# Pooled attention and soft MoE on one core: fewer and wider TensorE products, logit sums on VectorE, uneven weight rows moved

## The chip, the cores and the metric

The kernel runs on one core of a Trainium2 chip. The time is the device time of one execution in microseconds (us). A core has TensorE (PE; PEld is its weight load), VectorE (DVE), ScalarE (ACT), GpSimd (POOL), SyncE (SP) and 16 DMA engines, which all the transfers share. Instructions reach TensorE from a program in memory, and the profile lists the transfers that fetch it as a DMA queue of their own.

## The reference, cut to what matters

```python
B, H, S, D = 8, 8, 576, 64          # q, k, v: float32
k_p = k.reshape(B, H, 72, 8, D).mean(axis=3)       # pooled keys, v_p likewise
scores = q @ k_p.T / 8;  attn = softmax(scores, -1)
x = (attn @ v_p) as [4608 tokens, 512]             # heads side by side
logits = x @ phi                                   # phi: 512 x 32 slots
d = softmax(logits, over the 4608 tokens);  slot_input = d.T @ x     # 32 x 512
for e in range(8):                                 # 4 slots per expert
    slot_out[e] = relu(slot_input[e] @ w1[e]) @ w2[e]    # 512 x 1024, 1024 x 512
c = softmax(logits, over the 32 slots);  out = c @ slot_out          # 4608 x 512
```

## The kernel before, in words

**Data and loads.** The batches are taken two at a time: four pairs, `NP = 4`. A partition of a loaded tile holds 72 consecutive tokens of one head of one batch, so a pair's q, k or v fills 128 partitions with 72 x 64 values. All loads but half of the first one are issued by POOL and cast to bf16 on the way. They go in one order through one queue: k, q, phi and v of pair 0, k of pair 1, then q, v and the k after next, with w1 of the experts between them, then w2. `big` has four buffers for q, k and v (line 101), so a load waits until PE has done with the tile that lay there four loads earlier. The later halves of w2 take over the places of `big`, `qTa` and `xsa` when attention has finished with them. `load_w2` (line 115) brings experts 0 to 5 and half of expert 6; the loop at line 446 brings the rest of experts 6 and 7, cut into two column halves with four pieces each. Eight completion semaphores go round the loads that POOL issues: a load waits for the landing of the eighth load before it.

**Attention.** `prepare_kq` pools k: `pool_stage` (line 231) multiplies 8 strided slices by a matrix of 1/8 that keeps the partitions apart, in two parts of 4 and 5 rows of means, so 16 products; ACT copies the means out twice side by side; `turn_stage` (line 244) transposes them into `kp`; line 259 transposes q into `qTa`. `prepare_v` does the same for v, and line 281 multiplies one head's pooled v by `iphi`, the unit matrix beside phi of that head, so that a value row is followed by its share of the 32 logits. `score_unit` computes scores (line 290) and ACT their exponentials (line 292). `u_tile` (line 304) multiplies four heads' exponentials by values, and DVE divides by the sum (lines 309 and 315) into `xsa`. Preparing the next pair is a generator that is stepped between score units.

**Soft MoE.** `dispatch` (line 322) sums the eight heads' shares of the logits by eight products with the unit matrix, takes the exponential (line 323), and adds e x x into `G_ps` (line 326). It runs once per pair inside the next pair's attention, and for the last pair in two parts (tokens 0 to 4 and 5 to 8 of 9) after the loop. Then: `hidden` (line 475), `second_layer` (line 496) by expert as w2 lands, and from `begin` on the combine products (line 554), scaled by ACT (line 527) and DVE (line 529) and stored by SP (line 545).

**Order.** POOL keeps the written order throughout; for the other engines a scheduler orders the attention part, and the last part (from `hidden` on) is in the written order. `warm` (line 141) runs 8 products on zeros near the start.

**Uneven rows.** The load of w1 of expert 0 (line 106) is cut into partitions 0 to 111, 112 to 119 and 120 to 127; the other loads are not cut. A row of it is 4 x 1024 values, 8 KB as it lands.

Of the kernel before, what the change touches and what calls it, by code (L numbers as in the profile page):

```python
# [18 lines left out]
def kernel(  # L19
# [83 lines left out]

    def load_w1(e, n, parts=((0, 128),)):
        for p0, p1 in parts:
            nc.gpsimd.dma_start(out=w1_sb[p0:p1, e:e + n].rearrange("p e j f -> p e (j f)"),
                                in_=moe_w1[e:e + n].rearrange("e (p j) f -> p e (j f)", j=DJ)[p0:p1])

    w2_at = {}

    def load_w2(home, e, n, j0=0, j1=FJ):
# [3 lines left out]
        nc.gpsimd.dma_start(out=home[:, 0:n, j0 * DM:j1 * DM],  # L115
                            in_=moe_w2[e:e + n].rearrange("e (p j) d -> p e j d", j=FJ)[:, :, j0:j1].rearrange("p e j d -> p e (j d)"))

# [20 lines left out]

    def warm(n, ps):
        for _ in range(n):  # L140
            nc.tensor.matmul(out=ps, lhsT=zeros[:, 0:128], rhs=zeros, start=True, stop=True)

    warm_ps = ps_m.tile([128, 512], FP, name="warm_ps", tag="m")
    warm(8, warm_ps)
    dummy = consts.tile([128, 1], BF)
# [14 lines left out]

    iphi = consts.tile([128, H, XW], BF)
    with tc.tile_pool(name="tmp", bufs=1) as tmp:
        col = tmp.tile([128, A], FP, name="col")
        nc.vector.reduce_sum(out=col, in_=ident.rearrange("p (h a) -> p a h", a=A), axis=AX.X)
        head = tmp.tile([128, H], FP, name="head")
        nc.vector.reduce_sum(out=head, in_=ident.rearrange("p (h a) -> p h a", a=A), axis=AX.X)
        sel = tmp.tile([128, J, 2, A, J], BF, name="sel")
        nc.vector.memset(sel, 0.0)
        for j in range(J):
            nc.vector.tensor_copy(out=sel[:, j, :, :, j], in_=col.rearrange("p a -> p () a").to_broadcast([128, 2, A]))  # L170
        for r in range(2):
            rows = slice(r * D, (r + 1) * D)
            nc.vector.tensor_copy(out=iphi[rows, :, 0:D],
                                  in_=ident[rows, rows].rearrange("p d -> p () d").to_broadcast([D, H, D]))
# [9 lines left out]
        nc.scalar.copy(out=iphi[:, :, D:XW], in_=phi_ps)  # L184
    nc.vector.memset(siT, 0.0)
# [40 lines left out]
    def pool_stage(src, means, done):  # L226

        for i, (r0, r1) in enumerate(PARTS):
            ps = ps_m.tile([128, r1 - r0, D], FP, name="pool_ps", tag="m")
            for t in range(POOL):  # L230
                nc.tensor.matmul(out=ps, lhsT=pmat, rhs=src[:, r0 * POOL + t:r1 * POOL:POOL, :],  # L231
                                 start=(t == 0), stop=(t == POOL - 1))
            if i:
                done()
            nc.scalar.copy(out=means[:, r0:r1],
                           in_=ps.rearrange("p r d -> p r () d").to_broadcast([128, r1 - r0, means.shape[2], D]))
            yield

    def turn_stage(means, dst):
        dst = dst.rearrange("p n (r i) -> p r n i", r=NR)  # L240
        for r0, r1 in PARTS:
            ps = ps_m.tile([means.shape[2] * D, r1 - r0, BH, NI], BF, name="turn_ps", tag="m")
            for r in range(r0, r1):
                nc.tensor.transpose(out=ps[:, r - r0].rearrange("p n i -> p (n i)"),  # L244
                                    in_=means[:, r].rearrange("p c d -> p (c d)"), identity=ident)
            nc.vector.tensor_copy(out=dst[:, r0:r1], in_=ps)
            yield

    def prepare_kq(pair):
# [3 lines left out]
        kp[pair] = kvpool.tile([128, BH, SP], BF, name="kp", bufs=2)  # L253
        yield from turn_stage(means, kp[pair])
        for n, t0 in enumerate(range(0, NU, 6)):
# [14 lines left out]
    def prepare_v(pair):  # L270

        means = kvpool.tile([128, NR, 1, D], BF, name="vmeans")
        yield from pool_stage(v_sb[pair], means, lambda: after_v(pair))
        vpar = kvpool.tile([D, BH, SP], BF, name="vpar")
        yield from turn_stage(means, vpar)
        for b in range(2):
            for qd in range(2):
                ps = ps_m.tile([SP, HQ, XW], FP, name="v_ps", tag="m")
                for hh in range(HQ):
                    h = qd * HQ + hh  # L280
                    nc.tensor.matmul(out=ps[:, hh], lhsT=vpar[:, b * H + h], rhs=iphi[0:D, h], start=True, stop=True)
                nc.scalar.copy(out=vp[(2 * pair + b) % 5][:, qd * HQ:(qd + 1) * HQ, 0:XW], in_=ps)
                yield
# [33 lines left out]

    def dispatch(x, t0, t1, ps, ee):

        lg = ps_m.tile([128, 9, NS], FP, name="lg_ps", tag="m")[:, 0:t1 - t0]  # L320
        for h in range(H):
            nc.tensor.matmul(out=lg, lhsT=ident, rhs=x[:, t0:t1, h, D:XW], start=(h == 0), stop=(h == H - 1))  # L322
        nc.scalar.activation(out=ee[:, t0:t1], in_=lg.rearrange("p t s -> p t () s").to_broadcast([128, t1 - t0, NG, NS]), func=AF.Exp)  # L323
# [93 lines left out]
    load_w2(qTa, 4, 2)  # L417
    load_w2(xsa[:, 0:1], E - 2, 1, 0, CUT6)
    row_sums(0, 20, False)
# [116 lines left out]
    n = 0  # L536
# [99 lines left out]
```

## Time and profile before

| | |
|---|---|
| median of 3 runs | 176.71 us (175.95 to 176.75) |
| profiled execution | 175.6 us, its span 173.8 us |
| mean granted TensorE clock | 0.860 |
| busy: PE, DVE, ACT, POOL | 129.4, 90.9, 83.0, 20.3 us |
| DMA | 41.14 MB landed or stored in 10542 packets |

In the profile, L12 is line 12 of the kernel. A row of a group shows the engine, the operation, the tile written and those read, how often, then busy time, the mean of one in ns, and the idle time before it with what ended it. The page's digits are tenths of a fortieth of the span. An arrow `<-` after an idle time names what ended the wait.

### The profile page before, as it was taken

The page shows a single profiled execution, that of the slowest core. Times are in us where ns is not written, and L with a number is a line of the kernel's source. Part 1 is how long each engine was busy: PE and PEld are TensorE (multiplying, and loading weights), DVE is VectorE, ACT ScalarE, POOL GpSimd, SP SyncE. Part 2 cuts the span into 40 slices and gives each one's busy share as a digit, 9 for nine tenths or more (in the row PEclk, how much of TensorE's full clock was granted, in tenths as well). Part 3 has the DMA queues.
Part 4 walks back from the last instruction along what each step waited for, and adds up shares of the span by engine and source line. Part 5 has one row for each costly group of instructions (what it writes and reads, how often), then busy time and mean ns, then how long its engine had stood idle before and what let it go on. Part 6 is the DMA issues. An engine that isn't in the chain of part 4 may idle for free.

```text
span 173.8 us, 3094 instructions
## 1 busy us (share of the span) xinstructions
PE 129.4 (74%) x1239; PEld 76.9 (44%) x1240; DVE 90.9 (52%) x251; ACT 83.0 (48%) x155; POOL 20.3 (12%) x38
## 2 busy tenths in 40 slices
PE   5205889999999998979998897889973096798000
PEld 2003555766677665756765455534451032332000
DVE  4403242487777879758798668614260002599100
ACT  3200248976767469755698941450120004799000
POOL 7000111132110060100100004041010030000000
PEclk9955799999999999999999995555599569999755
DMA  5999999999999999999999999999999999999995
GB/s 190 246 221 219 218 218 209 218 216 214 218 212 207 216 216 216 214 221 215 215 213 213 215 222 217 217 213 211 217 219 221 202 193 197 308 359 409 437 437 226
DMA packets 10542, 41.14 MB, mean 237 GB/s; under 512 B 785, under 2 KB 6417, under 8 KB 6689
## 3 DMA queue, kind: packets, MB, share of 16 engines
q0 software_dynamic: 7072, 30.48, 86.4%
q1 hardware_dynamic: 3456, 10.49, 15.4%
q8 instruction: 9, 0.15, 0.3%
q14 instruction: 5, 0.03, 0.0%
HBM read 61.93 MB, written 9.44 MB: 411 GB/s over the span
## 4 chain that ended last, share of the span: by engine, by line
DMA 46%; PE 26%; issue 7%; DVE 5%; ACT 5%; POOL 2%; DVEq 0%; POOLq 0%; ACTq 0%
DMA qTa<-in_moe_w_dram 20%; DMA big<-in_q_dram 14%; DMA phi_f<-in_moe_phi_dram 7%; PE pool_ps L231 6%; DMA xsa<-in_moe_w_dram 6%; PE sc L290 5%; PE u_ps L304 4%; DVE w_sb L529 4%; PE q_ps L259 4%; ACT exa L292 3%; PE G_ps L326 2%; PE lg_ps L322 1%; PE turn_ps L244 1%; PE f_ps L554 1%; ACT qTa L263 1%
## 5 line engine op out<-in xcount | busy, mean ns | idle before, releaser
L292 ACT ACTIVATE exa<-sc 72x576 bf16<-72x576 f32 x64 | 39.1, 649 | 11.7 <-PE sc L290 11.3
L315 DVE TENSOR_TENSOR xsa<-u_ps,rec 128x384 bf16<-128x384 f32 x69 | 37.7, 552 | 1.4
L304 PE MATMUL u_ps<-vp,exa 72*128 72x97 bf16 (+1 forms) x320 | 27.1, 221 | 1.4 <-DVE xsa L315 1.3
L290 PE MATMUL sc<-qTa,kp 64*72 64x288 bf16 x128 | 23.2, 304 | 1.8 <-ACT exa L292 1.7
L304 PEld LDWEIGHTS <-exa 72*128 72x128 bf16 (+1 forms) x320 | 17.7, 106 | 10.7 <-DVE xsa L315 3.6
L231 PE MATMUL pool_ps<-big,pmat 128*128 128x320 bf16 (+1 forms) x128 | 20.2, 303 | 0.5 <-DMA big<-in_k_dram 0.5
L309 DVE RECIPROCAL rec<-u_ps 128x4 f32<-128x4 f32 x72 | 12.4, 176 | 15.1 <-PE u_ps L304 14.6
L231 PEld LDWEIGHTS <-pmat 128*128 128x128 bf16 x128 | 12.4, 103 | 5.0 <-DMA big<-in_k_dram 0.6
L259 PE MATMUL q_ps<-ident,big 128*128 128x128 bf16 x144 | 11.7, 219 | 2.3 <-DMA big<-in_q_dram 1.2
L554 PE MATMUL f_ps<-so,cT 128*128 128x512 bf16 (+1 forms) x42 | 10.2, 337 | 1.8 <-ACT w_sb L527 0.8
L290 PEld LDWEIGHTS <-kp 64*72 64x72 bf16 x128 | 8.5, 107 | 6.7 <-issue 2.3
L326 PE MATMUL G_ps<-xsa,ee 128*128 128x512 bf16 x36 | 10.7, 441 | 0.8 <-ACT ee L323 0.7
L259 PEld LDWEIGHTS <-big 128*128 128x128 bf16 x144 | 8.6, 97 | 5.1 <-issue 1.8
L265 DVE COPY qTa<-q_ps 128x768 bf16<-128x768 bf16 x16 | 8.9, 555 | 3.8 <-PE q_ps L259 3.6
L529 DVE TENSOR_SCALAR w_sb<-f_ps,recR 128x512 f32<-128x512 f32 (+1 forms) x17 | 10.5, 683 | 0.2
L529 DVE TENSOR_SCALAR so<-so_ps,recC 128x256 bf16<-128x256 f32 x2 | 1.0, 484 | 18.0 <-PE so_ps L496 18.0
L527 ACT ACTIVATE w_sb<-f_ps,recR 128x512 f32<-128x512 f32 (+1 forms) x17 | 9.6, 638 | 0.4 <-PE f_ps L554 0.2
L263 ACT COPY qTa<-q_ps 128x768 bf16<-128x768 bf16 x8 | 6.3, 793 | 6.3 <-PE q_ps L259 6.3
L446 POOL DMA_DIRECT2D xsa<-in_moe_w_dram x8 | 5.6, 706 | 31.2 <-DVE recR L365 9.2
L182 PE MATMUL phi_ps<-spread,sel 128*128 128x256 bf16 x4 | 1.4, 384 | 9.5 <-DVE spread L177 9.5
L527 ACT ACTIVATE so_a<-so_ps,recC 128x256 bf16<-128x256 f32 x2 | 0.9, 474 | 14.9 <-PE so_ps L496 14.8
L496 PEld LDWEIGHTS <-hT 128*32 128x32 bf16 x76 | 2.3, 102 | 12.2 <-issue 11.3
(90 smaller groups left out, 152.7 us busy)
## 6 DMA issues: line engine op xcount, KB each, us to landing
w_sb<-in_moe_w_dram POOLq DMA_DIRECT2D x3, 2048.0 KB, 37.6
big<-in_q_dram POOLq DMA_DIRECT2D x4, 1152.0 KB, 13.1
big<-in_v_dram POOLq DMA_DIRECT2D x4, 1152.0 KB, 16.9
big<-in_moe_w_dram POOLq DMA_DIRECT2D x2, 2048.0 KB, 44.9
big<-in_k_dram POOLq DMA_DIRECT2D x3, 1152.0 KB, 21.4
out_dram<-w_sb SPq DMA_DIRECT2D x2, 1536.0 KB, 8.7
out_dram<-w_sb SPq DMA_DIRECT2D x1, 2560.0 KB, 9.2
qTa<-in_moe_w_dram POOLq DMA_DIRECT2D x1, 2048.0 KB, 34.5
```

The source lines that it names most:

```text
L231: nc.tensor.matmul(out=ps, lhsT=pmat, rhs=src[:, r0 * POOL + t:r1 * POOL:POOL, :], start=(t == 0), stop=(t == POOL - 1))
L259: nc.tensor.transpose(out=ps[:, t].rearrange("p n i -> p (n i)"), in_=q_sb[pair][:, tt:tt + 2, :].rearrange("p t d -> p (t d)"), identity= ...
L265: nc.vector.tensor_copy(out=dst, in_=ps)
L290: nc.tensor.matmul(out=ps[:, r, 0:S // 2], lhsT=kp[pair][rows, n], rhs=qT[pair][rows, n].rearrange("p t i -> p (t i)"), start=True, stop=True)
L292: nc.scalar.activation(out=dst.rearrange("p r (i t) -> p r i t", t=NU), in_=ps[:, :, 0:S // 2].rearrange("p r (t i) -> p r i t", i=NI), fu ...
L304: nc.tensor.matmul(out=ps[rows, hh], lhsT=ex[b][:, hh].rearrange("p r t -> p (r t)")[:, c:c + rows.stop - rows.start], rhs=vp[(2 * pair + ...
L309: nc.vector.reciprocal(out=rec, in_=ps[:, :, XW])
L315: nc.vector.tensor_tensor(out=dst, in0=ps[:, :, 0:XW], in1=rec.rearrange("p h -> p h ()").to_broadcast([128, HQ, XW]), op=ALU.mult)
L326: nc.tensor.matmul(out=ps, lhsT=ee[:, t].rearrange("p g s -> p (g s)"), rhs=x[:, t, :, 0:D], start=(t == 0), stop=(t == 8))
L527: nc.scalar.activation(out=dst, in_=src, func=AF.Copy, scale=by)
L529: nc.vector.tensor_scalar(out=dst, in0=src, scalar1=by, scalar2=None, op0=ALU.mult)
L554: nc.tensor.matmul(out=ps, lhsT=tokens(n), rhs=so[:, cols], start=True, stop=True)
```

## The change

Six edits, of which the core is below.

1. `pool_stage`: rows of means 0 to 7 in 8 products of 512 columns, and row 8 in one product of 512 columns (8 tokens side by side), whose 8 columns per value DVE then adds (`reduce_sum`) and copies twice into the means. 9 products for 16, in each of 8 stages.
2. Values two heads at once: the means of v lie twice side by side as those of k do, `vpar` holds two heads on 128 partitions (written by four DVE copies in place of two), `iphi` becomes block-diagonal, and a product makes two heads. 8 products for 16 per pair.
3. Logit sums by a DVE `reduce_sum` for pairs 0, 1 and 3; pair 2 keeps the products.
4. `warm` and its 8 products go.
5. The load of w1 of expert 0 is one transfer; the load of the first half of expert 6's w2 is cut into 112, 8 and 8 partitions, with rows of 4 x 512 values, 8 KB as they are read and 4 KB as they land. The number of loads stays.
6. With the second edit come a memset of `iphi` and two ACT copies of phi in place of one.

TensorE's program has 2226 rows in place of 2482, weight loads included.

```diff
-    warm_ps = ps_m.tile([128, 512], FP, name="warm_ps", tag="m")
-    warm(8, warm_ps)
...
-            load_w1(0, 1, ((0, 112), (112, 120), (120, 128)))
+            load_w1(0, 1)
...
     def pool_stage(src, means, done):
-        for i, (r0, r1) in enumerate(PARTS):
-            ps = ps_m.tile([128, r1 - r0, D], FP, name="pool_ps", tag="m")
-            for t in range(POOL):
-                nc.tensor.matmul(out=ps, lhsT=pmat, rhs=src[:, r0 * POOL + t:r1 * POOL:POOL, :],
-                                 start=(t == 0), stop=(t == POOL - 1))
-            if i:
-                done()
-X
+        full = NR - 1
+        ps = ps_m.tile([128, full, D], FP, name="pool_ps", tag="m")
+        for t in range(POOL):
+            nc.tensor.matmul(out=ps, lhsT=pmat, rhs=src[:, t:full * POOL:POOL, :], start=(t == 0), stop=(t == POOL - 1))
+            if t == POOL // 2 - 1:
+                yield
+        rest = ps_m.tile([128, POOL, D], FP, name="rest_ps", tag="m")
+        nc.tensor.matmul(out=rest, lhsT=pmat, rhs=src[:, full * POOL:NR * POOL, :], start=True, stop=True)
+        done()
+        nc.scalar.copy(out=means[:, 0:full], in_=ps.rearrange("p r d -> p r () d").to_broadcast([128, full, 2, D]))
+        rsum = kvpool.tile([128, D], FP, name="rsum")
+        nc.vector.reduce_sum(out=rsum, in_=rest.rearrange("p t d -> p d t"), axis=AX.X)
+        nc.vector.tensor_copy(out=means[:, full], in_=rsum.rearrange("p d -> p () d").to_broadcast([128, 2, D]))
+        yield
...
+        def by_two(r0, r1, ps):
+            for c in range(2):
+                rows = slice(c * D, (c + 1) * D)
+                nc.vector.tensor_copy(out=dst[rows, r0:r1], in_=ps[rows, :, c:BH:2])
...
-                for hh in range(HQ):
-                    h = qd * HQ + hh
-                    nc.tensor.matmul(out=ps[:, hh], lhsT=vpar[:, b * H + h], rhs=iphi[0:D, h], start=True, stop=True)
+                for hh in range(0, HQ, 2):
+                    n = (qd * HQ + hh) // 2
+                    nc.tensor.matmul(out=ps[:, hh:hh + 2], lhsT=vpar[:, b * HQ + n], rhs=iphi[:, n],
+                                     start=True, stop=True)
...
-    def dispatch(x, t0, t1, ps, ee):
+    def dispatch(x, t0, t1, ps, ee, by_vector):
+        if by_vector:
+            lg = small.tile([128, 9, NS], FP, name="lg", bufs=1)[:, 0:t1 - t0]
+            nc.vector.reduce_sum(out=lg, in_=x[:, t0:t1, :, D:XW].rearrange("p t h c -> p t c h"), axis=AX.X)
+        else:
...
...
-        parts = dispatch(xs[pair], 0, 9, ps, ee)
+        parts = dispatch(xs[pair], 0, 9, ps, ee, pair < NP - 2)
...
-    load_w2(xsa[:, 0:1], E - 2, 1, 0, CUT6)
+    load_w2(xsa[:, 0:1], E - 2, 1, 0, CUT6, ((0, 112), (112, 120), (120, 128)))
...
-    first = dispatch(xs[NP - 1], 0, 5, G_ps, ee)
+    first = dispatch(xs[NP - 1], 0, 5, G_ps, ee, True)
...
-    second = dispatch(xs[NP - 1], 5, 9, G_ps, ee)
+    second = dispatch(xs[NP - 1], 5, 9, G_ps, ee, True)
```

More of the change, by code (lines that the diff above doesn't have):

```diff
@@ L102, in load, with load_w1, load_w2 @@
         return t.rearrange("p (t d) -> p t d", d=D)
[L104 to L107, printed above, removed]
+    def load_w1(e, n):
+        nc.gpsimd.dma_start(out=w1_sb[:, e:e + n].rearrange("p e j f -> p e (j f)"),
+                            in_=moe_w1[e:e + n].rearrange("e (p j) f -> p e (j f)", j=DJ))
     w2_at = {}
-    def load_w2(home, e, n, j0=0, j1=FJ):
+    def load_w2(home, e, n, j0=0, j1=FJ, parts=((0, 128),)):
         for i in range(n):
@@ L114, in load_w2 @@
                 w2_at[e + i, j] = home[:, i, j * DM:(j + 1) * DM]
-        nc.gpsimd.dma_start(out=home[:, 0:n, j0 * DM:j1 * DM],
-                            in_=moe_w2[e:e + n].rearrange("e (p j) d -> p e j d", j=FJ)[:, :, j0:j1].rearrange("p e j d -> p e (j d)"))
+        src = moe_w2[e:e + n].rearrange("e (p j) d -> p e j d", j=FJ)[:, :, j0:j1].rearrange("p e j d -> p e (j d)")
+        for p0, p1 in parts:
+            nc.gpsimd.dma_start(out=home[p0:p1, 0:n, j0 * DM:j1 * DM], in_=src[p0:p1])
     CUT = 4 * POOL * D
@@ L172 @@
             rows = slice(r * D, (r + 1) * D)
-            nc.vector.tensor_copy(out=iphi[rows, :, 0:D],
-                                  in_=ident[rows, rows].rearrange("p d -> p () d").to_broadcast([D, H, D]))
+            nc.vector.tensor_copy(out=iphi[rows, :, r, 0:D],
+                                  in_=ident[rows, rows].rearrange("p d -> p () d").to_broadcast([D, HQ, D]))
         spread = tmp.tile([128, J, H, NS], BF, name="spread")
@@ L183 @@
                              start=(j == 0), stop=(j == J - 1))
-        nc.scalar.copy(out=iphi[:, :, D:XW], in_=phi_ps)
+        for r in range(2):
+            rows = slice(r * D, (r + 1) * D)
+            nc.scalar.copy(out=iphi[rows, :, r, D:XW], in_=phi_ps[rows, r:H:2])
     nc.vector.memset(siT, 0.0)
@@ L245, in turn_stage @@
                                     in_=means[:, r].rearrange("p c d -> p (c d)"), identity=ident)
-            nc.vector.tensor_copy(out=dst[:, r0:r1], in_=ps)
+            put(r0, r1, ps)
             yield
@@ L253, in prepare_kq @@
         kp[pair] = kvpool.tile([128, BH, SP], BF, name="kp", bufs=2)
-        yield from turn_stage(means, kp[pair])
+        dst = kp[pair].rearrange("p n (r i) -> p r n i", r=NR)
+        yield from turn_stage(means, lambda r0, r1, ps: nc.vector.tensor_copy(out=dst[:, r0:r1], in_=ps))
         for n, t0 in enumerate(range(0, NU, 6)):
@@ L316, in u_tile @@
                                     in1=rec.rearrange("p h -> p h ()").to_broadcast([128, HQ, XW]), op=ALU.mult)
-    def dispatch(x, t0, t1, ps, ee):
-        lg = ps_m.tile([128, 9, NS], FP, name="lg_ps", tag="m")[:, 0:t1 - t0]
-        for h in range(H):
-            nc.tensor.matmul(out=lg, lhsT=ident, rhs=x[:, t0:t1, h, D:XW], start=(h == 0), stop=(h == H - 1))
+    def dispatch(x, t0, t1, ps, ee, by_vector):
[3 more added lines that the diff above has]
+        else:
+            lg = ps_m.tile([128, 9, NS], FP, name="lg_ps", tag="m")[:, 0:t1 - t0]
+            for h in range(H):
+                nc.tensor.matmul(out=lg, lhsT=ident, rhs=x[:, t0:t1, h, D:XW], start=(h == 0), stop=(h == H - 1))
         nc.scalar.activation(out=ee[:, t0:t1], in_=lg.rearrange("p t s -> p t () s").to_broadcast([128, t1 - t0, NG, NS]), func=AF.Exp)
```

19 lines of the change are left out of this document (7 added, 12 removed).

## The prediction

> **What bounds the kernel now.** I read the page's parts 1 to 3 first, then the chain that ended last, then stretches of the span.
>
> ```profile
> span 173.8 us, 3094 instructions
> PE 129.4 (74%) x1239; PEld 76.9 (44%) x1240; DVE 90.9 (52%) x251; ACT 83.0 (48%) x155; POOL 20.3 (12%) x38
> DMA  5999999999999999999999999999999999999995
> GB/s 190 246 221 219 218 218 209 218 216 214 218 212 207 216 216 216 214 221 215 215 213 213 215 222 217 217 213 211 217 219 221 202 193 197 308 359 409 437 437 226
> q0 software_dynamic: 7072, 30.48, 86.4%
> q8 instruction: 9, 0.15, 0.3%
> HBM read 61.93 MB, written 9.44 MB: 411 GB/s over the span
> ```
>
> PE is busiest, but the DMA row is the one without a gap: nine tenths or more in all but the first and last slice. The loads land at about 215 GB/s as bf16, that is twice that as read float32. At 2 x 215 the 61.93 MB read take 144 us, and that is nearly all of the time before the output phase. The chain in order of time says the same:
>
> ```profile
> 44.19 6.20 issue
> 50.41 24.46 DMA big<-in_q_dram
> ...
> 104.12 34.49 DMA qTa<-in_moe_w_dram
> 138.68 0.49 issue
> 139.17 9.62 DMA xsa<-in_moe_w_dram
> 148.84 0.31 PE so_ps L496 x3
> ```
>
> A 2 MB load takes 34.49 us from its issue at 104.12 because it stands behind others; by itself, at 215 GB/s, it is 9.8 us. The loads of w2 are therefore queued up some 25 us ahead, and a PE or POOL that reaches 104.12 sooner only makes the queue longer. From 148.84 to the end (25.0 us) run the last products, the scaling and the stores, in code which the change leaves alone. How far PE stands ahead of the loads is told by the stretches and one wait:
>
> ```profile
> 40.00:75.00 35.00, 32.86 (x380) 23.01 (x379) 26.47 (x76) 24.08 (x44) 5.56 (x9) 1.00 1.03 215
> 75.00:104.00 29.00, 27.61 (x293) 17.45 (x293) 21.84 (x61) 20.54 (x36) 0.70 (x1) 1.00 1.03 216
> 104.00:121.00 17.00, 14.29 (x116) 8.08 (x119) 9.48 (x31) 5.16 (x16) 4.79 (x7) 0.52 1.03 215
> 132.00:139.00 7.00, 0.34 (x4) 0.13 (x7) 0.00 (x0) 0.00 (x0) 0.00 (x0) 0.75 1.03 213
> PE so_ps L496 <- DMA qTa<-in_moe_w_dram: 6.9, 1, 6.9
> ```
>
> The columns are the stretch, its length, busy time of PE, PEld, DVE, ACT, POOL, clock, DMA share, GB/s. PE is nearly full from 40 to 104 us, DVE three quarters full. Then PE runs out of work and waits 6.9 us for w2. That wait is the reserve of the whole compute part: attention and what follows it may end up to 6.9 us later before the end moves, and not a moment of ending earlier is worth anything.
>
> **The products that go.** Rows of PE, and pieces of the chain with several products in a row:
>
> ```profile
> L231 PE MATMUL pool_ps<-big,pmat 128*128 128x320 bf16 (+1 forms) x128 | 20.2, 303 | 0.5 <-DMA big<-in_k_dram 0.5
> 31.93 2.07 PE pool_ps L231 x16
> 31.11 0.29 PE v_ps L281 x4
> 75.43 0.49 PE lg_ps L322 x4
> 1.99 3.60 PE L141 MATMUL warm_ps<-hT 128*128 128x512 bf16 x8 [1.99 <-DVE ones L151]
> ```
>
> Pooling streams 4608 columns before and after (8 x 256 + 8 x 320; 9 x 512). If columns set its 2.07 us, nothing is saved; if the count does, 7/16 or 0.9 us per stage, 0 to 7.2 us in eight. I take 0.1 per stage, since 2.07 us for 16 products of 288 columns on average lies close to a constant time per column. Four value products took 0.29 us; two of double width cost between 0.15 and 0.29, so 16 such groups save 0 to 2.3 us. The logit products of pairs 0 and 1 take 2 x 0.49 us a pair, 2 us together. All this is PE time that ends in the 6.9 us wait, or in the earlier ones for q and k: its worth is 0. The warm-up ran at 1.99 us and its PE time is beside the first load. Does its going leave PE slower when it first works?
>
> ```profile
> 12.00:15.00 3.00, 0.00 (x0) 0.00 (x0) 0.36 (x2) 0.00 (x0) 0.00 (x0) 0.50 1.02 222
> 16.00:17.00 1.00, 1.00 (x7) 0.63 (x5) 0.07 (x1) 0.37 (x1) 0.00 (x0) 0.50 1.05 221
> 19.00:20.00 1.00, 1.00 (x9) 0.58 (x6) 0.00 (x0) 0.12 (x1) 0.00 (x0) 0.79 1.02 212
> ```
>
> The clock had fallen to 0.50 before the first pooling anyway and rose in it, at about 19 us; the warm-up bought nothing that was left by then. Bounds 0 and, if all 3.57 us of pooling stayed at its slow rate, 0.3 us; I take 0.
>
> **The work that DVE gets.** No row shows a sum of this size. The nearest:
>
> ```profile
> L164 DVE TENSOR_REDUCE col<-ident 128x16 f32<-128x128 bf16 x1 | 0.4, 379 | 0.0
> L529 DVE TENSOR_SCALAR w_sb<-f_ps,recR 128x512 f32<-128x512 f32 (+1 forms) x17 | 10.5, 683 | 0.2
> L149 DVE TENSOR_SCALAR pmat<-ident 128x128 bf16<-128x128 bf16 x1 | 0.2, 189 | 0.0
> L246 DVE COPY vpar<-turn_ps 64x512 bf16<-64x512 bf16 (+1 forms) x8 | 3.4, 437 | 2.9 <-PE turn_ps L244 2.9
> ```
>
> The sum over row 8 reads 512 values: 0.68 us by the pass over 512 values from PSUM, 1.5 by four times the small sum; I take 0.7, with 0.19 for the copy: 7.1 us in eight stages (13.5 at the high price). The extra `vpar` copies: 0 to 0.9 us a pair, I take 0.4, so 1.6 (3.6). The logit sums of pairs 0 and 1 read 2304 values: 3.1 us by 4.5 passes of 0.683, 6.8 by eighteen small sums. Those of pair 3 read 1280 and 1024 values: 3.1 together, or 6.8. In all DVE gets 18 us (38 at the high prices) on 90.9.
>
> Where it lands: from 40 to 75 us DVE has 8.5 us idle and gets three stages, one logit sum and a `vpar` set, 6.2 us. From 75 to 104 it has 7.2 us idle and gets one stage, one sum and a set, 4.4 us. Both fit. After 104 the two sums stand in line before `G_ps`: 3.1 us more, less the 2 us of products they replace. Some 1 to 3 us of the reserve of 6.9 go; worth at the end 0. The Trainium skill, page "VectorE: DVE Perf Modes", section "Rules for kernel authors", speaks against the move: it calls `tensor_reduce` the slowest VectorE operation and advises against it on a hot path. At one value a cycle and the clock that the skill gives (0.96 GHz), a sum over 2304 values would be an estimated 2.4 us, a little below the price I use; no row of this run shows one so large.
>
> **The order on POOL.** The number of loads is 32 before and after, but the two cuts move from the tenth place to the 22nd. Each load waits for the landing of the eighth before it, so the pieces of w2 wait for others than before:
>
> ```profile
> 119.47 0.74 POOL L446 DMA_DIRECT2D xsa<-in_moe_w_dram  x1 [3.19 <-DMA big<-in_moe_w_dram]
> 129.45 0.74 POOL L446 DMA_DIRECT2D xsa<-in_moe_w_dram  x1 [9.24 <-DVE recR L365]
> 139.17 0.74 POOL L446 DMA_DIRECT2D xsa<-in_moe_w_dram  x1 [8.98 <-DMA qTa<-in_moe_w_dram]
> 141.64 0.59 POOL L446 DMA_DIRECT2D xsa<-in_moe_w_dram  x1 [1.73 <-DMA xsa<-in_moe_w_dram]
> xsa<-in_moe_w_dram POOLq DMA_DIRECT2D x1, 64.0 KB, 7.5
> big<-in_k_dram POOLq DMA_DIRECT2D x1, 640.0 KB, 7.6
> ```
>
> The four pieces of the second half were issued at 119.47, 129.45, 139.17 and 141.64. Now the first waits for `qTa` (139.17) and the second for the first of the three new transfers (about 141.3); the third and fourth follow at 142.1 and 142.8. They are wanted later: the last 64 KB landed 7.5 us after 141.64, at 149.1, and the half's 768 KB take some 4 us, so it starts to move at 145.1, its second piece at 146.4, the third at 147.8. From issue to first byte it cannot take more than about 2.1 us: the first load, 640 KB, landed 7.6 us after issue behind 1 MB of float32, and the two move in about 5.5 us. So the second piece is ready at 143.4, 3 us early. Worth 0. Behind these waits nothing is queued on POOL but the pieces themselves.
>
> **What the DMA engines lose or gain.** TensorE's program is fetched through the same 16 engines: queue q8, 9 packets, 0.15 MB, 16 KB each. 0.3% of 16 x 173.8 us is 8.3 us, 0.93 us a packet, on one engine. The program loses 256 rows of 2482, which at 64 bytes a row (0.15 MB over 2482) is one packet. A load has landed when its slowest engine has; so the packet is worth between 0.93/16 = 0.06 us (all engines equal) and 0.93 us (it was on the slowest). The page "Runtime: NRT & Kernel Launch" of the Trainium skill, section "Instruction fetch mechanics", has 256 instructions to a block of 16 KiB and calls the cost of a block mostly hidden; the size agrees with the row. By that rule this term would be 0.
>
> The uneven rows only make sense as a tilt: eight partitions cannot be shared by 16 engines, so a piece gives some engines a row that others lack.
>
> ```profile
> 90.00:104.00 14.00, 12.61 (x128) 7.43 (x126) 10.25 (x30) 10.61 (x19) 0.00 (x0) 1.00 1.03 215
> ```
>
> At 215 GB/s one of 16 engines lands an 8 KB row in 8192/(215/16) = 0.61 us. If both pieces go to the same eight engines, these get two rows more than the others, 1.2 us before and, with 4 KB rows, 0.6 us after; if they go to different ones, nothing changes. Which engines also fetch the program the page does not tell, so the term lies between -0.6 and +0.6 us. A smaller tilt beside one fetch less is nearer to even than a large one; I take -0.15, and for the fetch -0.2.
>
> **The sum.** Products, warm-up, DVE, POOL: 0 each on the path. Fetch -0.2, tilt -0.15: -0.35 us. The profiled execution took 175.6 us (span 173.8), 1.1 below the median of the runs shown, 176.71; taken off that, 176.71 - 0.35 = 176.4 us.
>
> **The rivals.**
> - *VectorE becomes the bound, slower.* For it: DVE in line with PE in 40 to 104, sums that no row prices. At the high prices 40 to 75 gets 11 to 13 us on 8.5 idle, 75 to 104 gets 9.4 on 7.2, and the sums after 104 put up to 5 us into the line: 4 + 2 + 5 = 11 us against the reserve of 6.9. It decides from 6.9 us; halfway, 3 us are left over: 179.5 us. Against it: all prices must be high, and PE saves some us in the same stretches. 0.10.
> - *The last pieces come late.* If a load needs over 5 us from issue to first byte, the second half starts its second piece late; at 6 us the stream stands still for 1 us: 177.5 us. Against it: the bound of 2.1 us above. 0.04.
> - *Slowest engine relieved in full.* If the dropped packet and one 4 KB row (0.3 us) both came off the engine that ended last, the stream ends 0.93 + 0.3 = 1.2 us sooner: 175.5 us. 0.09.
> - *Tilt the wrong way.* If the large tilt was what balanced the fetches, halving it costs up to 0.6 us, less 0.06: 177.2 us. 0.05.
>
> **How the numbers follow.** The forecast has the remaining 0.72. Within 0.5% (0.9 us, about what a measurement of this kernel can tell from no change; the three runs differ by as much) lie the forecast but 0.03, the wrong tilt, and 0.01 each of the first two rivals: 0.76. Faster by more: 0.09 + 0.03 = 0.12. Slower by more: 0.09 + 0.03 = 0.12. The range reaches from the relieved engine, 175.3, to the start of the VectorE case, 177.8, and leaves out some 0.15.
>
> **What would show it.** Right: the DMA row without gaps, q8 with 8 packets, the wait of so_ps for `qTa` between 3 and 7 us, the last `xsa` piece landing near 148.5. Wrong: that wait gone and DVE at nine tenths in 40 to 104 (VectorE); a DMA digit under 9 near 145 (pieces late); sums over 0.7 and 3.1 us would show the DVE step mis-sized even if the end stands.

## The result: 182.43 us, 3.2% slower

| | before | after |
|---|---|---|
| median of 4 runs each | 176.73 us (175.95 to 177.1) | 182.43 us (181.09 to 183.06) |
| ratio, 95% interval | | 1.0318 [1.0246, 1.0390] |
| profiled execution, its span | 175.6 us, 173.8 us | 182.91 us, 181.1 us |
| first product of the second layer (`so_ps<-big`) | 129.9 us | 146.6 us |
| last scaling before the first store (`so_a`) | 145.12 us | 152.32 us |

The forecast was 176.4 us with a range to 177.8, so the result lies outside. These are the rows of the changed kernel's page that answer to those shown of before:

```profile
span 181.1 us, 2869 instructions
PE 127.7 (70%) x1111; PEld 69.9 (39%) x1112; DVE 109.0 (60%) x280; ACT 83.2 (46%) x148; POOL 20.3 (11%) x38
PEclk9999999999999659999759995795555799999755
DMA  5999999999999999999999999999999980699995
GB/s 204 229 222 216 222 210 220 219 207 220 212 219 216 215 218 214 220 210 219 214 221 212 215 219 214 217 214 217 217 217 196 194 121 0 231 342 448 428 417 220
q8 instruction: 8, 0.13, 0.3%
```

Up to its 32nd slice the DMA row has no gap: the weights still arrive at the same rate and end at the same time. But now an 8, a 0 and a 6 follow, where before there were nines: a slice is 4.53 us, so from 149.4 to 154 us the DMA engines have nothing to do. The loads no longer set when the output phase begins; the compute does. PEclk, the granted clock of TensorE in tenths, has a 6 and a 5 from 58.9 to 67.9 us, and a 7 and a 5 from 86.0 to 95.1, where before it had nines:

```profile
PEclk9955799999999999999999995555599569999755
```

The chain that ended last says it too. First its shares by engine, then its pieces around the first logit sum, and its end (start, length, what):

```profile
PE 45%; DVE 20%; ACT 14%; DMA 6%; issue 6%; POOL 1%; DVEq 0%; ACTq 0%; POOLq 0%
```

```profile
56.35 0.18 DVE rec L320
56.53 3.93 DVE lg L333
60.47 0.02 issue
60.49 1.17 ACT ee L338
61.66 0.05 issue
61.71 4.02 PE G_ps L341 x9
...
146.65 2.70 PE so_ps L511 x48
...
152.32 0.48 ACT so_a L542
```

Before, the three DMA pieces shown alone made 68.6 of the 98 us from 50.4 to 148.8; now DMA holds 6% of the chain, and the logit sum, the exponential and the nine `G_ps` products stand in it one behind the other. No wait of `so_ps` for `qTa` is left, which the prediction took for the reserve. In the timeline of PE, DVE and ACT one sees what the sum does there:

```profile
56.45 4.00 DVE L333 TENSOR_REDUCE lg<-xsa 128x288 f32<-128x2304 bf16 x1
...
60.37 0.55 DVE L326 TENSOR_TENSOR xsa<-u_ps,rec 128x384 bf16<-128x384 f32 x1
...
60.97 0.48 PE L315 MATMUL u_ps<-vp,exa 72*128 72x97 bf16 x4 [1.98 <-DVE xsa L326]
...
61.71 4.02 PE L341 MATMUL G_ps<-xsa,ee 128*128 128x512 bf16 x9 [0.25 <-ACT ee L338]
```

DVE takes up nothing else while the sum runs. For these 4.00 us the scaling of `u_ps` into `xsa` of the next pair stands behind it (60.37); PE runs out of free `u_ps` tiles and stops for 1.98 us, works for 0.48, and waits again for `ee`. The stretches beside it (start and end, length, busy PE, PEld, DVE, ACT, POOL, clock, DMA share, GB/s) show what goes with the stop:

```profile
56.00:58.00 2.00, 1.97 (x28) 1.39 (x28) 1.81 (x3) 1.88 (x5) 0.00 (x0) 1.00 1.03 214
58.00:60.00 2.00, 0.54 (x4) 0.23 (x4) 2.00 (x1) 1.73 (x3) 0.00 (x0) 1.00 1.01 213
60.00:62.00 2.00, 0.78 (x5) 0.40 (x5) 2.00 (x7) 1.16 (x1) 0.00 (x0) 0.65 1.04 218
62.00:64.00 2.00, 2.00 (x6) 0.76 (x5) 0.91 (x3) 0.00 (x0) 0.00 (x0) 0.50 1.04 219
```

PE is busy for 1.32 of the 4 us from 58 to 62, the granted clock falls to 0.50, and the nine `G_ps` products that follow take 4.02 us, where the first nine took 2.10 before. By groups (busy, mean ns, idle before and its releasers), first before, then after:

```profile
L304 PE MATMUL u_ps<-vp,exa 72*128 72x97 bf16 (+1 forms) x320 | 27.1, 221 | 1.4 <-DVE xsa L315 1.3
L326 PE MATMUL G_ps<-xsa,ee 128*128 128x512 bf16 x36 | 10.7, 441 | 0.8 <-ACT ee L323 0.7
```

```profile
L341 PE MATMUL G_ps<-xsa,ee 128*128 128x512 bf16 x36 | 15.7, 605 | 4.5 <-ACT ee L338 4.5
L315 PE MATMUL u_ps<-vp,exa 72*128 72x97 bf16 (+1 forms) x320 | 27.6, 226 | 7.5 <-DVE xsa L326 6.6
L333 DVE TENSOR_REDUCE lg<-xsa 128x288 f32<-128x2304 bf16 (+2 forms) x4 | 12.2, 3046 | 1.1 <-ACT xsa L324 1.1
L237 DVE TENSOR_REDUCE rsum<-rest_ps 128x64 f32<-128x512 f32 x8 | 5.5, 692 | 9.0 <-PE rest_ps L233 8.8
```

`G_ps` takes 5.0 us more; its wait for `ee` grew by 3.8, and that of `u_ps` for `xsa` from 1.3 to 6.6. These 14.1 us are most of the 16.7 us by which `so_ps<-big` is late. It grows with each pair: `G_ps` began at 57.2, 79.7, 99.1 and 112.9 us before, and 4.6, 9.4, 13.8 and 15.6 us later after. The sum of pair 2 is left on TensorE, and still its `G_ps` loses another 4.4 us: what lies behind the sums, the low clock and the new pooling among it, adds to the delay.

### The profile page after: what moved, and what is told of

Its sections match the earlier page's. It is cut to its first block, busy times and chain, and to the rows that moved or that the text cites. A ratio compares the mean times of both kernels' runs of the same rounds, so it can differ in the third digit from the quotient of the medians.

```text
span 181.1 us, 2869 instructions
## 1 busy us (share of the span) xinstructions
PE 127.7 (70%) x1111; PEld 69.9 (39%) x1112; DVE 109.0 (60%) x280; ACT 83.2 (46%) x148; POOL 20.3 (11%) x38
## 4 chain that ended last, share of the span: by engine, by line
PE 45%; DVE 20%; ACT 14%; DMA 6%; issue 6%; POOL 1%; DVEq 0%; ACTq 0%; POOLq 0%
PE G_ps L341 8%; PE pool_ps L229 7%; DVE lg L333 7%; DMA phi_f<-in_moe_phi_dram 6%; PE u_ps L315 5%; PE sc L301 5%; ACT exa L303 5%; PE q_ps L261 4%; DVE xsa L326 4%; DVE w_sb L544 4%; PE h_ps L490 3%; PE so_ps L511 2%; ACT kmeans L235 2%; PE turn_ps L245 2%; ACT ee L338 2%
## 5 line engine op out<-in xcount | busy, mean ns | idle before, releaser
L315 PEld LDWEIGHTS <-exa 72*128 72x128 bf16 (+1 forms) x320 | 19.3, 109 | 19.0 <-issue 7.8
L301 PE MATMUL sc<-qTa,kp 64*72 64x288 bf16 x128 | 21.6, 310 | 3.2 <-ACT exa L303 2.9
L229 PE MATMUL pool_ps<-big,pmat 128*128 128x512 bf16 x64 | 18.7, 411 | 0.4 <-ACT qTa L265 0.2
L341 PE MATMUL G_ps<-xsa,ee 128*128 128x512 bf16 x36 | 15.7, 605 | 4.5 <-ACT ee L338 4.5
L320 DVE RECIPROCAL rec<-u_ps 128x4 f32<-128x4 f32 x72 | 12.1, 175 | 9.6 <-PE u_ps L315 9.1
L261 PE MATMUL q_ps<-ident,big 128*128 128x128 bf16 x144 | 12.8, 234 | 1.0 <-DVE qTa L267 0.3
L333 DVE TENSOR_REDUCE lg<-xsa 128x288 f32<-128x2304 bf16 (+2 forms) x4 | 12.2, 3046 | 1.1 <-ACT xsa L324 1.1
L261 PEld LDWEIGHTS <-big 128*128 128x128 bf16 x144 | 9.8, 106 | 3.0 <-issue 2.3
L237 DVE TENSOR_REDUCE rsum<-rest_ps 128x64 f32<-128x512 f32 x8 | 5.5, 692 | 9.0 <-PE rest_ps L233 8.8
L341 PEld LDWEIGHTS <-ee 128*128 128x128 bf16 x36 | 4.5, 138 | 12.2 <-issue 6.5
L229 PEld LDWEIGHTS <-pmat 128*128 128x128 bf16 x64 | 6.0, 104 | 6.0 <-issue 2.0
```

Of the source, the lines that this page charges most:

```text
L229: nc.tensor.matmul(out=ps, lhsT=pmat, rhs=src[:, t:full * POOL:POOL, :], start=(t == 0), stop=(t == POOL - 1))
L261: nc.tensor.transpose(out=ps[:, t].rearrange("p n i -> p (n i)"), in_=q_sb[pair][:, tt:tt + 2, :].rearrange("p t d -> p (t d)"), identity= ...
L301: nc.tensor.matmul(out=ps[:, r, 0:S // 2], lhsT=kp[pair][rows, n], rhs=qT[pair][rows, n].rearrange("p t i -> p (t i)"), start=True, stop=True)
L315: nc.tensor.matmul(out=ps[rows, hh], lhsT=ex[b][:, hh].rearrange("p r t -> p (r t)")[:, c:c + rows.stop - rows.start], rhs=vp[(2 * pair + ...
L320: nc.vector.reciprocal(out=rec, in_=ps[:, :, XW])
L333: nc.vector.reduce_sum(out=lg, in_=x[:, t0:t1, :, D:XW].rearrange("p t h c -> p t c h"), axis=AX.X)
```

## The experiments

Ratios are to runs of the kernel before on the same chip beside them (medians 175.88 to 176.10 us). "Start" is the first `so_ps<-big` in the profiled execution, which is one of the runs; 129.9 before, 146.6 after.

### One part undone, or one part alone

**Sums back on TensorE** (after, all else kept):

```diff
-        parts = dispatch(xs[pair], 0, 9, ps, ee, pair < NP - 2)
+        parts = dispatch(xs[pair], 0, 9, ps, ee, False)
...
-    first = dispatch(xs[NP - 1], 0, 5, G_ps, ee, True)
-    second = dispatch(xs[NP - 1], 5, 9, G_ps, ee, True)
+    first = dispatch(xs[NP - 1], 0, 5, G_ps, ee, False)
+    second = dispatch(xs[NP - 1], 5, 9, G_ps, ee, False)
```

> The changed kernel, but all logit sums by TensorE again. Theory 1 (the long VectorE sums stand in line between the value products and G_ps, stop TensorE, and its clock falls): the first second-layer product, at 146.7 us after the change and 129.9 before, comes back by 8 to 13 us, and the time to 176 to 178 us. Theory 2 (the new pooling stage, with one long ScalarE copy and a VectorE sum before the transposes, costs over a us in each of 8 stages): the time stays at 180 us or more.

Measured: 176.67 us, 1.0023 [0.9988, 1.0059], start 135.2. The loss is gone: without the DVE sums the change costs nothing that stands clear of the noise. The first theory was right in both numbers.

**The sums alone** (before, with edit 3):

```diff
+            lg = small.tile([128, 9, NS], FP, name="lg", bufs=1)[:, 0:t1 - t0]
+            nc.vector.reduce_sum(out=lg, in_=x[:, t0:t1, :, D:XW].rearrange("p t h c -> p t c h"), axis=AX.X)
```

> The kernel before with nothing but the logit sums of pairs 0, 1 and 3 on VectorE. Theory 1: second layer 9 to 13 us later than 129.9, the wait for the fifth and sixth experts' weights gone, 178 to 182 us. Theory 2: second layer under 6 us later, inside the wait of 6.9 us, 176.7 us.

Measured: 177.38 us, 1.0054 [1.0014, 1.0095], start 142.0. In the profiled execution the compute is 12.1 us late, and the wait for `qTa` is gone, as the first theory had it; but the time stays under its 178 to 182 us. Five of the ten runs took 176.4 to 176.9 us and five, the profiled one among them, 177.9 to 178.4. Its groups, with the shapes apart, give the same lengths as in the changed kernel:

```profile
L322 DVE TENSOR_REDUCE lg<-xsa 128x288 f32<-128x2304 bf16 x2 | 8.1, 4028 | 0.0
L322 DVE TENSOR_REDUCE lg<-xsa 128x160 f32<-128x1280 bf16 x1 | 2.3, 2280 | 0.0
L322 DVE TENSOR_REDUCE lg<-xsa 128x128 f32<-128x1024 bf16 x1 | 1.9, 1865 | 1.1 <-ACT xsa L313 1.1
```

**The pooling alone**, and **the values alone** (before, with edit 1, or with edit 2 and the `iphi` that goes with it):

```diff
+        rest = ps_m.tile([128, POOL, D], FP, name="rest_ps", tag="m")
+        nc.tensor.matmul(out=rest, lhsT=pmat, rhs=src[:, full * POOL:NR * POOL, :], start=True, stop=True)
...
+                    nc.tensor.matmul(out=ps[:, hh:hh + 2], lhsT=vpar[:, b * HQ + n], rhs=iphi[:, n],
```

> The kernel before with nothing but the pooling in 9 products. Theory 1: second layer 2 to 5 us later, hidden by the wait of 6.9 us, 176.7 us with the wait at 2 to 5 us. Theory 2: second layer over 9 us later and 178 us or more.

> The kernel before with nothing but the values two heads at once. Both theories: no change, 176.7 us, second layer within 2 us of 129.9.

Measured: 176.58 us, 1.0008 [0.9976, 1.0039], start 133.5; and 176.37 us, 1.0002 [0.9968, 1.0035], start 132.1. Each is hidden, though the starts are 3.6 and 2.2 us later. The slowdown has no single owner, and the times show it: the sums alone cost 0.5%, pooling and values without them 0.2%, and all together 3.2%. The sums bring the compute past the reserve, and what delays it beside them then costs time.

How the delay splits is less sure, because executions differ. Two kernels that are the same up to the output phase, the sums on TensorE above and the variant with two fillers below, start at 135.2 and 132.1 us (132.0 with three fillers). Their clock rows:

```profile
PEclk9999999999999999558999985895799996999555
PEclk9999999999999999999999956756996879999555
```

In the first, the clock is at 0.50 from 70.0 to 78.8 us, with no logit sum on DVE and no stop of PE over 0.31 us from 60 to 71 us; in the second, with the same stops, it holds. The second `G_ps` begins at 86.84 and 83.17 us. In the profiled execution of the sums alone the clock fell in the same way at about 48 us, before the first sum (55.76), so its 12.1 us are not the sums' alone. Pooling holds up better: with it, alone or beside the values, the first `G_ps` began at 59.2 to 59.4 us in four profiles, 57.2 before. With the values alone the first two `G_ps` began 0.5 and 0.6 us sooner than before, and the 2.2 us came later; no run here shows that they belong to that edit.

### What about the sums: which, how long, how laid out

**Only the last pair's sums by DVE** (the first of the three new lines above alone) and **only the first two pairs'** (the other two alone).

> The changed kernel with the logit sums of pairs 0 and 1 by TensorE again, those of pair 3 still on VectorE. If the two sums inside attention are most of it: the first second-layer product comes back from 146.7 to 137 to 140 us, which is about the 9.5 us that the end leaves, and the time is 176.5 to 177.5 us. If the sums of the last pair matter more, it stays over 142 us and the time over 178.

> The changed kernel with the logit sums of pair 3 by TensorE again, those of pairs 0 and 1 on VectorE. If the two sums inside attention are most of it: second layer back by 2 to 4 us only, 179 to 181 us. If the last pair's matter more: back by over 6 us, under 178 us.

Measured: 177.69 us, 1.0119 [1.0051, 1.0186], start 142.3 (its profiled execution, 179.9 us, lies above the median of its runs); and 180.17 us, 1.0228 [1.0160, 1.0297], start 143.5. Taking the first two pairs' sums off DVE gives back 2.0 of the 3.2%, taking the last pair's off 0.9% (there the intervals overlap). The second fits its expectation. The first lies between its two, with a start over 142 and a time under 178; in its profiled execution the clock fell at about 48 us, where no logit sum ran on DVE.

**The same sums as adds.** Three passes of `tensor_tensor` in place in `xsa`, each adding the upper half of the heads to the lower:

```diff
-            nc.vector.reduce_sum(out=lg, in_=x[:, t0:t1, :, D:XW].rearrange("p t h c -> p t c h"), axis=AX.X)
+            for n in (4, 2):
+                nc.vector.tensor_tensor(out=x[:, t0:t1, 0:n, D:XW], in0=x[:, t0:t1, 0:n, D:XW], in1=x[:, t0:t1, n:2 * n, D:XW], op=ALU.add)
+            nc.vector.tensor_tensor(out=lg, in0=x[:, t0:t1, 0, D:XW], in1=x[:, t0:t1, 1, D:XW], op=ALU.add)
```

> The changed kernel with each logit sum over eight heads made by three passes of additions (4, 2 and 1 heads with as many others, in bf16 in the place of xsa) in place of one reduction; the order of the sums and their rounding differ. If the length of the block that VectorE takes is what counts: the three passes take 1.5 to 3 us for 4.0, the second layer starts 3 to 8 us sooner than 146.7, and the time falls to 176.5 to 180 us, the shorter the better. If any VectorE sum at that place costs the same: no change, 182 us.

Measured: 176.53 us, 1.0033 [1.0006, 1.0060], start 137.3. The groups of this run:

```profile
L334 DVE TENSOR_TENSOR xsa<-xsa 128x1152 bf16<-128x1152 bf16 x2 | 1.5, 728 | 0.0
L335 DVE TENSOR_TENSOR lg<-xsa 128x288 f32<-128x288 bf16 x2 | 0.9, 458 | 0.0
L334 DVE TENSOR_TENSOR xsa<-xsa 128x576 bf16<-128x576 bf16 x2 | 0.9, 450 | 0.0
```

728 + 450 + 458 ns = 1.64 us for 4.0: the same sums, still on DVE, and 9.3 of the 16.7 us are back, within what the theory of the block's length had.

**The same reduction in nine pieces**, one per row of tokens. Nothing is saved: the sums take 14.6 us for 12.2, and DVE is busy for 109.5 us, 109.0 in the changed kernel:

```diff
+            for t in range(t0, t1):
+                nc.vector.reduce_sum(out=lg[:, t - t0], in_=x[:, t, :, D:XW].rearrange("p h c -> p c h"), axis=AX.X)
```

> The changed kernel with each logit sum over VectorE cut into one sum per token row (nine of 256 values where there was one of 2304; the same values, the same total). Theory 'one long block stands in VectorE's line' (the 4.0 us sum keeps xsa, and with it u_ps, G_ps and the clock, waiting): the pieces let other VectorE work in between, so the first so_ps<-big starts at about 138 to 142 us for 146.6 and the time is 177 to 179 us. Theory 'the amount counts' (12 us more VectorE work, wherever it lies, because the row's logits need all of it before G_ps): so_ps<-big stays at 145 to 148 us and the time at 181 to 184 us. If the nine pieces together take well over 4.0 us, the second also holds, with the excess added.

Measured: 177.22 us, 1.0057 [1.0021, 1.0093], start 140.2. Its timeline of DVE and its waits (what waited, in all, times, longest) show the difference:

```profile
49.49 0.55 DVE L334 TENSOR_REDUCE lg<-xsa 128x32 f32<-128x256 bf16 x1
49.96 0.54 DVE L326 TENSOR_TENSOR xsa<-u_ps,rec 128x384 bf16<-128x384 f32 x1
...
56.18 2.54 DVE L334 TENSOR_REDUCE lg<-xsa 128x32 f32<-128x256 bf16 x5
```

```profile
PE u_ps L315 <- DVE xsa L326: 4.7, 11, 0.9
PE G_ps L342 <- ACT ee L339: 1.8, 3, 0.8
```

Four of the nine pieces of pair 0 move ahead, between the last scalings of that pair, and five stay in a block. The time falls by 5.2 us and the start by 6.4 although the sums take a little longer, so the amount of work alone is not the cause: what counts is the length of the block in DVE's line and in front of `ee`. The five in the block and a clock that still fell stand for part of what is left; how much was not tried.

**Fillers for the clock.** Ten products on zeros beside each sum of pairs 0 and 1, placed ahead of the `u_ps` that stops:

```diff
+                for _ in range(10):
+                    nc.tensor.matmul(out=idle, lhsT=ident, rhs=zeros, start=True, stop=True)
```

> The changed kernel with 10 more products on zeros beside each sum of pairs 0 and 1, which nobody reads, so that TensorE is not idle while VectorE sums. If the fall of the clock is part of the price: G_ps then runs its nine products in about 2 us for 4.0, the granted clock stays at 1.00 in 60 to 68 us, and the second layer starts 3 to 6 us sooner, the time 178 to 181 us. If the wait alone is the price: second layer as before or 1 to 4 us later, 182 us or more.

Measured: 181.04 us, 1.0279 [1.0221, 1.0337], start 144.3.

```profile
60.00:62.00 2.00, 0.81 (x10) 0.62 (x9) 2.00 (x8) 1.60 (x2) 0.00 (x0) 1.00 1.04 218
62.00:64.00 2.00, 1.85 (x9) 0.80 (x9) 1.63 (x5) 0.64 (x2) 0.00 (x0) 1.00 1.04 219
```

At the first sum the clock holds at 1.00 where it fell to 0.65 and 0.50, and the first nine `G_ps` take 2.12 us for 4.02: the low clock doubles them. At the second it fell in spite of the fillers (0.51 in 88 to 90 us, nine `G_ps` in 3.61 us). The start is 2.3 us sooner, which is neither expectation, and less than two executions of one kernel can differ; the fillers took 2.33 us of PE at the first sum themselves. The interval overlaps that of the changed kernel. So what the fallen clock is worth in time is not shown.

### The reserve, read off all of these

| kernel | start, us | ratio |
|---|---|---|
| before | 129.9 | 1 |
| values alone | 132.1 | 1.0002 |
| pooling alone | 133.5 | 1.0008 |
| sums on TensorE | 135.2 | 1.0023 |
| sums as adds | 137.3 | 1.0033 |
| reduction in nine pieces | 140.2 | 1.0057 |
| sums alone | 142.0 | 1.0054 |
| last pair's sums by DVE | 142.3 | 1.0119 |
| first two pairs' sums by DVE | 143.5 | 1.0228 |
| fillers | 144.3 | 1.0279 |
| the change | 146.6 | 1.0318 |

The ratios are from medians and each start from one execution, so a row can be off by some 3 us. Up to a start of 137.3 us the time moves by 0.3% at most, and then it climbs with the delay. The bend follows from two rows: in the changed kernel, where no load holds it up, `so_a` comes 5.7 us behind the start (146.65 to 152.32), and 5.7 to 5.8 us in the other five with a start past 140. Before, it came at 145.12, set by the loads:

```profile
145.12 0.47 ACT L527 ACTIVATE so_a<-so_ps,recC 128x256 bf16<-128x256 f32 x1 [14.77 <-PE so_ps L496]
```

So the start may be as late as 139.4, which is a reserve of 9.5 us, not 6.9. 16.7 - 9.5 = 7.2 us is the delay of `so_a` and agrees with the spans (181.1 - 173.8 = 7.3).

### The transfers and the warm-up alone

Before, with edits 4 and 5 (2466 rows; the 2474 below leave out the weight loads that go with the eight products):

```diff
-    warm(8, warm_ps)
...
+            load_w1(0, 1)
...
+    load_w2(xsa[:, 0:1], E - 2, 1, 0, CUT6, ((0, 112), (112, 120), (120, 128)))
```

> The kernel before with only the transfer part of the change: the uneven rows of 8 partitions moved from the piece of w1 to the 4 KB piece of w2, and the eight warm-up products left out (2474 rows of TensorE's program for 2482; the fetches stay at nine). The prediction gave the smaller tilt -0.15 us (bounds -0.6 to +0.6) and the warm-up 0: 175.7 to 175.9 us beside a kernel before of 175.9, the last load landing at 148.65 us. Rival 'the large tilt balanced the fetches': up to +0.6 us, landing at 149.2 us or later. Rival 'the warm-up mattered': the first pooling ends later than 19.9 us, by up to 0.3 us, and nothing at the end. If the landing does not move at all, the 0.03 to 0.4 us that the other variants gained there came with the dropped fetch.

Measured: 176.24 us, 1.0013 [0.9993, 1.0033]. Its chain has the product that waits for the last load, which began at 148.84 before:

```profile
142.43 6.47 DMA xsa<-in_moe_w_dram
148.90 0.04 issue
148.94 0.31 PE so_ps L490 x3
```

The tilt gave nothing (0.1 us the other way, less than runs of one kernel differ), and the fetches stay at nine. Pooling with and without the warm-up starts at 15.6 and 15.7 us, and its copies at 18.0 and 18.1: the warm-up was indeed worth nothing. The clock row is no help there: without the warm-up it reads 1.00 from the start, yet 15 products of the first pooling took 3.58 us, and 3.55 us before, at 0.50. A mean granted clock is therefore not to be compared between a kernel with `warm` and one without.

### What the mended kernels lose in the output phase

With the sums as adds, or on TensorE, the compute is within the reserve, and still the ratio was 1.0033 or 1.0023. In both the clock fell to 0.50 at about 146 us, in the second only until 149. The guess was that PE had too little to do while the last pieces of w2 came in (busy for 2.2 of the 4 us from 142 in the first, 2.0 in the second). So products on zeros went behind the first two pieces, three each, then two each:

```diff
+        if i < 2:
+            busy(3)
```

> The changed kernel with each logit sum as three passes of adds in place (as in a_tree, 176.53 us, 1.0033) and, behind each of the first two pieces of the second half's work, three more filler products on TensorE, so that it does not stand idle from 142 to 146 us. Theory 'the adds cured the compute and what is left over is the clock in the output phase' (granted 0.50 in 148 to 156 us in a_tree): clock 1.00 from 145 us on, and the time falls by 0.6 to 1.0 us against a_tree, to 175.3 to 175.8 us, ratio 0.996 to 0.999. Theory 'the output phase is set by its stores whatever the clock': the clock is 1.00 but the time stays at 176.3 to 176.7 us. Last load landing at 148.4 to 148.6 us in both.

> The changed kernel with all logit sums back on TensorE (as in a_sums_pe, 176.67 us, 1.0023) and the same six filler products as a_tree_busy. By the clock theory 175.5 to 176.0 us, ratio 0.996 to 0.999; by the store theory 176.4 to 176.8 us. If this one gains and a_tree_busy does not, the adds still cost something on the path.

Measured: 177.81 us, 1.0091 [1.0063, 1.0119], and 177.26 us, 1.0063 [1.0034, 1.0091]. Both came out longer than without fillers, by 0.6 and 0.4% (in the second the intervals overlap), against both theories, and `so_a` came at 145.74 and 145.77 us where it was at 144.89 and 144.87: the fillers held it up. Then two instead of three:

> As a_tree_busy (177.81 us, 1.0091), with two filler products instead of three behind each of the first two pieces of the second half's work: 0.50 us of fillers in gaps of 0.78 and 0.71 us, so that so_a is not held back. If the half clock in the output phase (0.50 from 146 to 156 us in a_tree) is what a_tree lost: clock 1.00 there, so_a at 144.9 us, time 175.3 to 175.9 us, ratio 0.996 to 0.999. If the stores set the output phase whatever the clock: 176.2 to 176.7 us, 1.001 to 1.004, as a_tree. If the fillers still hold so_a back, 176.7 to 177.8 us.

> As a_sums_pe_busy (177.26 us, 1.0063) with two fillers instead of three. Clock theory: 175.4 to 176.0 us, 0.996 to 0.999; store theory: 176.2 to 176.7 us, 1.001 to 1.004, as a_sums_pe (176.67 us, 1.0023).

Measured: with adds 175.85 us, 1.0000 [0.9971, 1.0028]; on TensorE 176.88 us, 1.0042 [1.0017, 1.0067]. In the first, `so_a` is at 144.88 and the clock stays up. Here is one stretch of the output phase in four kernels: as adds, as adds with two fillers, on TensorE, on TensorE with two fillers.

```profile
152.00:154.00 2.00, 2.00 (x9) 1.00 (x8) 1.51 (x4) 1.97 (x5) 0.00 (x0) 0.50 0.54 186
152.00:154.00 2.00, 2.00 (x9) 0.80 (x8) 1.87 (x5) 2.00 (x5) 0.00 (x0) 1.00 0.94 316
152.00:154.00 2.00, 1.92 (x10) 0.82 (x9) 1.87 (x5) 2.00 (x5) 0.00 (x0) 1.00 0.52 178
152.00:154.00 2.00, 1.97 (x8) 0.80 (x8) 1.88 (x4) 2.00 (x5) 0.00 (x0) 1.00 0.69 234
```

With adds, the stores ran dry at half clock (DMA share 0.54) and not at full clock (0.94), but the intervals of the two runs overlap. On TensorE they ran dry at full clock as well. In the last of the four the clock is at 1.00 from 142 to 160 us, and `so_a` at 145.24 is only 0.12 us behind that of the kernel before, which lost nothing; still it takes 0.4% more, close to what the theory of the stores had. There the first store of the second half took SP 1.36 us to issue, 0.34 before. So the clock is not the whole reason, and what these kernels lose in the output phase stays open. The best version, with adds and two fillers, equals the kernel before within the noise; none beat it.

## Why the prediction was wrong, step by step

- **The loads as the bound, worth nothing to end earlier: right** for what it was read from. The stream of weights ends as before, and every variant whose compute stays within the reserve comes out within 0.5%, but for the two with three fillers, which held up `so_a` themselves.
- **"Both fit": the step that failed.** It set DVE's added work against DVE's idle time in a stretch, and from that had the compute end 1 to 3 us later. It ended 16.7 us later, on a reserve of 9.5. The amount was right: DVE's busy time rose by 18.1 us, and 18 had been forecast. Nor was DVE full: busy 28.0 of 35 and 23.68 of 29 us in those stretches, under the nine tenths that the prediction named as the sign of this case:

```profile
40.00:75.00 35.00, 30.55 (x283) 18.08 (x280) 28.00 (x73) 21.80 (x37) 4.77 (x8) 0.90 1.03 216
75.00:104.00 29.00, 25.12 (x231) 15.34 (x228) 23.68 (x59) 16.89 (x30) 1.41 (x2) 0.88 1.03 216
```

  DVE's idle time lies scattered between short scalings that PE needs back at once. A 4 us block does not fit into it, whatever its sum: the same sums in pieces start the second layer 6.4 us sooner, as short adds 9.3 us, off DVE 11.4 us. The prediction asked who is busy and not who is queued behind the block.
- **The sum over 2304 values: mis-sized.** 3.1 us taken, 4.0 measured; pair 3's two 4.2 us together, not 3.1. It stayed within its bounds. The Trainium skill, page "VectorE: DVE Perf Modes", section "The perf-mode tier table (the rule you actually need)", has a single-rate program for `tensor_reduce` and a double-rate one for `tensor_tensor` in bf16. The adds agree: 1152 values in 0.73 us, where one value a cycle at the skill's 0.96 GHz would be an estimated 1.2 us. For the reduction the same rate would be an estimated 2.4 us, and the measured 4.0 decides. The advice of its section "Rules for kernel authors", to consider restructuring, was right here: the prediction named the section, and then set it aside for a price.
- **No term for the clock.** Stops of PE were priced at their length. `G_ps` took 5.0 us more over its four stages, nearly 4 of them in the first two at the low clock. What this is worth at the end was not separated.
- **"PE savings worth 0": too kind.** Hardly any were left. Value products take 246 ns for 205 at double width, 4.6 us in all for 4.8; pooling takes 18.7 us and 3.1 for the extra product, 20.2 before. The copy of the means is now one of 1.01 us behind all products, where two of about 0.6 and 0.69 partly ran beside them. Pooling delays the first `G_ps` by some 2 us in four profiles; a delay by the values is not shown. Which of the copies does it was not tried.
- **The reserve: 6.9 taken, 9.5 measured.** The wait for `qTa` is only the first of the waits for loads; the pieces behind it hold slack too.
- **The rest sums (0.7 taken, 0.69), the POOL order, and the warm-up: right.** The second half's pieces came without a gap.
- **Fetch and tilt: -0.35 us on the path, not seen.** The program did shrink to 8 packets. Where the last load sets the pace with 8 packets (sums as adds with two fillers), the product behind it began at 148.59, against 148.84 before and 148.94 with the tilt alone. That is the size forecast, but runs of one kernel differ by more, and no median shows a gain. So no run shows the -0.15 and -0.2 us of the sum.
- **The rival "VectorE becomes the bound"** had the right place and was given 0.10 and 179.5 us. It came nearer, by another mechanism than busy time, and at 4.0 us a sum, well under the high price of 6.8 that it was thought to need. Its time does not follow from its own numbers: of 11 us on a reserve of 6.9, halfway leaves 2 us and not 3.

## What to carry to other kernels

Cost an operation that moves to an in-order engine by the longest block that it puts in front of that engine's short, urgent work, and by who waits for these, not by the engine's idle share. When several hidden parts delay the same path, add up their delays against one reserve, and measure the reserve to the last wait, not the first. If a block must go there, cut it or shorten it first: the same change cost 3.2% with the sums in one block, 0.6% in pieces, 0.3% as adds and 0.2% with the sums left on TensorE. And read a delay from more than one execution: two of kernels alike up to that place differed by 3 us.

## What the runs showed of the hardware

- `tensor_reduce` over bf16 in SBUF, with the summed axis strided: 573 ns for 256 values, 1865 for 1024, 4028 for 2304, by estimate some 0.15 us and 1.7 ns a value. Over 512 float32 values in PSUM it took 692 ns. Whether type, place or stride makes the difference was not tried.
- At the first sum of the changed kernel the clock fell although PE stood idle for at most 1.98 us at a time; it was busy for 1.32 of 4 us. The Trainium skill, page "TensorE: Matmul & The Clock Gate", section "Why this matters for your kernels", warns of idle gaps of over about 3 us. Here it also fell with no stop over 0.31 us (sums on TensorE, 70.0 us), and held in another execution with the same stops. So a stop is not needed for a fall, and what sets it off no run here shows.
- Fillers against that are neither free nor sure: three behind a piece where two fitted moved `so_a` from 144.88 to 145.74 us, and ten beside a sum held the clock at the first sum and not at the second (0.51).
